# Attention, gated MLP and bilinear MLP in one kernel: six blocks of three row tiles become seven blocks of 2, 3, 3, 3, 3, 2 and 2

## The chip, the cores and the metric

The kernel runs on one core of one Trainium2 chip. The metric is the device time of one execution in microseconds (us): the median of several runs, and beside it one profiled execution, whose trace gives each instruction's start and end on each engine. TensorE is called PE in the trace (PEld is its weight loads), VectorE DVE, ScalarE ACT, GpSimd POOL, and SyncE, which issues most transfers here, SP.

## The reference, cut to what matters

```
q, k, v: (4, 8, 576, 64) fp32          # batch, heads, tokens, head size
scores = q @ k^T / 8
kth    = the 32nd largest score of each row
attn   = softmax(scores where score >= kth)
x      = (attn @ v), heads side by side # 2304 tokens x 512
h      = x @ w_in;  g = h * sigmoid(h); x2 = g @ w_out    # 512 -> 2048 -> 512
out    = ((x2 @ w1) * (x2 @ w2)) @ w3 @ w_out2            # 512 -> 1024 -> 1024 -> 512
```

The weights reach the kernel as 64-bit numbers, seen as pairs of 32-bit words.

## The kernel before, in words

The 2304 tokens are 18 row tiles of 128. They are worked in blocks of consecutive row tiles (the list BLOCKS). A block has two parts: its attention (8 heads), and then its MLP, one chain through all the weights with T = 128 x tiles columns in each matmul.

**Attention.** The (head, row tile) combinations of a block are taken two at a time: a pair. Each pair has a slot of 7 ticks in a plan. In its slot VectorE finds the 32 largest scores of both row tiles: four MAX8 (L462) and three MATCH_REPLACE8 (L466) per row tile, over 576 columns. A slot earlier TensorE has made the scores and ScalarE has copied them out (L435). A slot later ScalarE masks and takes exponentials (L482, L488), POOL normalises (L514), and when a head's row tiles are through, TensorE transposes (L569 or L572/L574) and multiplies with v (L600 or L609). A block of three row tiles has 12 slots, a block of two has 8. In blocks 0 and 1 (NATIVE: `j < 2`) attention runs in plain fp32, which needs no preparation of k and v. From block 2 on, q, k, v and the probabilities are split into a high and a low fp32r part by ScalarE and POOL, and TensorE multiplies both (two matmuls of 288 columns for half a row tile's scores, L431 and L432). The split k and v of a batch are written to DRAM if a later block needs the same batch.

**MLP.** 48 pieces of weights of 512 KB (high and low part of 128 x 512 weights) go by in order. Each product is three matmuls (L671 high x high, L672 high x low, L673 low x high). A block's MLP has 16 steps of the first part, 8 of the second: 48 pieces x 12 = 576 matmuls of T columns. The last product (w3 and the second w_out are multiplied beforehand, "folded") has 24 matmuls of 512 columns for each row tile (L792). Between the matmuls of a step the results go through tanh on ScalarE (L708), the gate on VectorE (L713), the cast to the high part on ScalarE (L685) and the subtraction of it on POOL (L686).

**Conversion.** The first time round, the weights are converted from 64-bit words: beside block 0's attention the 24 pieces to be folded, and beside block 1's attention, in step with block 0's MLP, the 48 pieces (ACT L140, L143, L136, L201, POOL L138, L156, L202, DVE L150, L153). They are written to scratch DRAM. For every later block the MLP streams all 48 pieces back (L206, issued by SP, which waits in order for a free buffer).

**Order.** The MLP of block j is spread over the ticks of the attention of block j+1. All engines take their instructions in the order that the plan gives. MLP j+1 starts only when MLP j has been issued to its end; the last MLP has no attention beside it.

Of the kernel before, what the change touches and what calls it, by code (L numbers as in the profile page):

```python
# [16 lines left out]
TOPK = 32  # L17

SHIFT = 2.0 ** -112
BLOCKS = [3, 3, 3, 3, 3, 3]  # L20
LAG = 1
WT = 3
AHEAD = 4
# [29 lines left out]
def attention_moe_moe2_kernel(  # L53
# [25 lines left out]
    scale = 1.0 / float(D) ** 0.5  # L79
    NB = len(BLOCKS)  # L80

# [17 lines left out]
    def bank(why=""):  # L99
        if not free_banks:  # L100
            raise RuntimeError(f"no bank: {sorted(held.values())}")
        b = free_banks.pop(0)
        held[id(b)] = why
        return b
# [174 lines left out]
    t0 = 0  # L279
    for n in BLOCKS:  # L280
        blocks.append((t0, n * 128))
# [18 lines left out]
    for j in range(NB):  # L300
        seq = [(j, h, i) for h in range(H) for i in range(BLOCKS[j])]
        pairs += [seq[n:n + 2] for n in range(0, len(seq), 2)]
# [234 lines left out]
    def plan_av(j, h):  # L537
# [22 lines left out]
        for kc in range(KC):  # L560
            u = {}

            def tr(u=u, kc=kc):
                u["ps"] = ps = bank("pt")
                for i in range(BLOCKS[j]):
                    p = st["p"][i]
# [350 lines left out]
```

## Time and profile before

| | |
|---|---|
| median of 3 runs | 1204.77 us (1200.64 to 1205.74) |
| the profiled execution | 1202.4 us, of which its span (first to last instruction) 1200.6 us |
| PE busy | 1149.0 us (96%), 6216 matmuls |
| DVE busy | 931.9 us (78%) |
| ACT busy | 850.1 us (71%) |
| POOL busy | 724.9 us (60%) |
| moved by DMA | 254.27 MB |

A matmul's recorded duration is longer than the time from its start to the start of the next one, since matmuls overlap. So what a matmul costs in a stream is read from two starts, not from its duration. A busy share is an average over stages that have different limits.

### The profile page before, as it was taken

What the parts mean: (1) busy time and instruction counts of PE and PEld (TensorE: products, weight loads), DVE (VectorE), ACT (ScalarE), POOL (GpSimd) and SP (SyncE); (2) the same over time, 40 slices, a digit from 0 to 9 for tenths busy, and PEclk for the clock granted to TensorE, in tenths of its full rate; (3) what the DMA queues carried; (4) which work ended last, traced back from release to release, by engine and by line L of the source; (5) the groups of instructions that cost most, each with busy time, mean ns of one, the idle gap of its engine ahead of it and who ended that gap; (6) DMA issues with size and microseconds to landing.
All of it is one profiled execution on the core that took longest, in us unless ns stands there. A gap on an engine that the chain in (4) does not pass through costs nothing.

```text
span 1200.6 us, 19669 instructions
## 1 busy us (share of the span) xinstructions
PE 1149.0 (96%) x6216; PEld 990.4 (82%) x6216; DVE 931.9 (78%) x2136; ACT 850.1 (71%) x1907; POOL 724.9 (60%) x744
## 2 busy tenths in 40 slices
PE   7799959899989999999999999999999999999997
PEld 4354535678868889989899999999999999999997
DVE  7888898999897988898889978977888998601100
ACT  6676777789897677887788778878967878642221
POOL 4454461777879367786688766677755766542231
PEclk9999989999999999999999999999999999999999
DMA  9652381678867357676678666888866775538640
GB/s 244 207 152 68 107 274 49 235 245 279 270 238 256 140 183 226 209 232 217 201 253 290 220 232 206 287 301 260 293 224 205 237 233 185 186 106 288 239 166 26
DMA packets 122504, 254.27 MB, mean 212 GB/s; under 512 B 40224, under 2 KB 63264, under 8 KB 122400
## 3 DMA queue, kind: packets, MB, share of 16 engines
q1 hardware_dynamic: 114336, 225.75, 58.3%
q10 hardware_dynamic: 8064, 27.27, 5.9%
q8 instruction: 49, 0.80, 0.3%
q14 instruction: 55, 0.45, 0.1%
HBM read 206.31 MB, written 46.66 MB: 211 GB/s over the span
## 4 chain that ended last, share of the span: by engine, by line
PE 83%; ACT 7%; DMA 4%; POOL 2%; issue 2%; DVE 1%; SPq 1%; ACTq 0%; POOLq 0%; DVEq 0%
PE bank L671 16%; PE bank L672 16%; PE bank L673 15%; PE bank L792 8%; PE bank L600 4%; PE bank L569 4%; PE bank L429 4%; PE bank L609 4%; PE bank L572 3%; PE bank L431 2%; PE bank L432 2%; PE bank L238 2%; PE bank L243 2%; DMA raw<-in_w_in_dram 1%; ACT e L482 1%
## 5 line engine op out<-in xcount | busy, mean ns | idle before, releaser
L462 DVE MAX8 top<-wk 128x8 f32<-128x576 f32 x432 | 320.5, 753 | 3.7
L686 POOL TENSOR_TENSOR gl<-gf,gh 128x384 fp32r<-128x384 f32 x144 | 148.3, 1031 | 140.0 <-ACT gh L685 131.3
L466 DVE MATCH_REPLACE8 wk<-top,wk 128x576 f32<-128x576 f32 x288 | 213.7, 744 | 0.0
L435 ACT ACTIVATE st<-bank 128x288 f32<-128x288 f32 (+1 forms) x320 | 128.1, 414 | 59.0 <-PE bank L432 30.3
L590 POOL TENSOR_TENSOR pl<-pf,ph 128x384 fp32r<-128x384 f32 x128 | 129.3, 1017 | 60.3 <-ACT ph L588 51.9
L462 DVE MAX8 top<-st 128x8 f32<-128x576 f32 x144 | 108.2, 754 | 48.6 <-ACT st L435 48.0
L671 PE MATMUL bank<-x2h,wt 128*128 128x384 f32 x384 | 131.6, 347 | 2.8 <-ACT x2h L730 2.8
L671 PE MATMUL bank<-xh,wt 128*128 128x384 f32 x384 | 130.5, 343 | 3.4 <-DVE gf L713 1.3
L672 PE MATMUL bank<-gl,wt 128*128 128x384 f32 x384 | 131.9, 344 | 1.2 <-POOL gl L686 0.7
L672 PE MATMUL bank<-x2l,wt 128*128 128x384 f32 x384 | 130.6, 340 | 1.3 <-POOL x2l L731 1.0
L673 PE MATMUL bank<-x2h,wt 128*128 128x384 f32 x384 | 129.4, 337 | 0.0
L673 PE MATMUL bank<-gh,wt 128*128 128x384 f32 x384 | 129.1, 336 | 0.0
L673 PE MATMUL bank<-xh,wt 128*128 128x384 f32 x384 | 129.0, 336 | 0.0
L672 PE MATMUL bank<-xl,wt 128*128 128x384 f32 x384 | 128.9, 336 | 0.0
L713 DVE SCALAR_TENSOR_TENSOR gf<-th,bank 128x384 f32<-128x384 f32 x96 | 52.3, 548 | 81.3 <-ACT th L708 77.1
L488 ACT ACTIVATE e<-e,nb 128x576 f32<-128x576 f32 x144 | 111.5, 779 | 0.0
L482 ACT ACTIVATE e<-st,nt 128x576 f32<-128x576 f32 x144 | 105.0, 777 | 8.3 <-DVE nt L474 6.5
L466 DVE MATCH_REPLACE8 wk<-top,st 128x576 f32<-128x576 f32 x144 | 106.7, 744 | 0.0
L156 POOL TENSOR_TENSOR w<-w,raw 128x512 f32<-128x512 f32 x48 | 66.5, 1386 | 59.8 <-DVE w L150 21.2
L685 ACT CAST gh<-gf 128x384 fp32r<-128x384 f32 x144 | 74.6, 519 | 39.3 <-DVE gf L780 24.3
L587 ACT COPY pf<-bank 128x384 f32<-128x384 f32 (+1 forms) x160 | 77.4, 484 | 33.6 <-PE bank L572 26.8
L514 POOL TENSOR_SCALAR e<-e,rc 128x640 f32<-128x640 f32 x96 | 75.8, 802 | 36.5 <-DVE rc L498 32.8
(95 smaller groups left out, 2974.9 us busy)
## 6 DMA issues: line engine op xcount, KB each, us to landing
wt<-scr SPq DMA_DIRECT2D x240, 512.0 KB, 4.2
scr<-wt ACTq DMA_DIRECT2D x48, 512.0 KB, 4.0
raw<-in_w_dram SPq DMA_DIRECT2D x24, 512.0 KB, 5.1
k<-kk SPq DMA_DIRECT2D x16, 576.0 KB, 5.1
kk<-k SPq DMA_DIRECT2D x16, 576.0 KB, 5.0
raw<-in_w3T_dram SPq DMA_DIRECT2D x16, 512.0 KB, 4.5
raw<-in_w_in_dram SPq DMA_DIRECT2D x16, 512.0 KB, 5.4
raw<-in_w_out_dram SPq DMA_DIRECT2D x16, 512.0 KB, 5.1
```

What stands on the lines that cost most here:

```text
L435: nc.scalar.activation(out=tiles[n][r0:r1, m, cs], in_=ps[r0:r1, 0:HS], func=ACTF.Copy, scale=scale)
L462: nc.vector.max(out=st["top"][:, i, r * 8:r * 8 + 8], in_=st["s" if r == 0 else "wk"][:, i])
L466: nc.vector.match_replace(out=st["wk"][:, i], in_to_replace=st["top"][:, i, r * 8:r * 8 + 8], in_values=st["s" if r == 0 else "wk"][:, i], ...
L482: nc.scalar.activation(out=e[:, 0:S], in_=st["s"][:, i], func=ACTF.Prelu, bias=st["nt"][:, i:i + 1], alpha=BELOW)
L488: nc.scalar.activation(out=e, in_=e, func=ACTF.Exp, bias=st["nb"][:, i:i + 1], accum_out=st["sm"][:, i, 0:1])
L587: nc.scalar.copy(out=pf[f], in_=u["ps"][f, 0:T])
L590: nc.gpsimd.tensor_sub(out=pl[f], in0=pf[f], in1=ph[f])
L671: nc.tensor.matmul(ps, lhsT=wh, rhs=rh, start=first, stop=False)
L672: nc.tensor.matmul(ps, lhsT=wh, rhs=rl, start=False, stop=False)
L673: nc.tensor.matmul(ps, lhsT=wl, rhs=rh, start=False, stop=last)
L686: nc.gpsimd.tensor_sub(out=u["l"], in0=full, in1=u["h"])
L792: nc.tensor.matmul(oacc[t], lhsT=a[:, ts], rhs=b[:, i, :], start=(i == 0 and x == 0), stop=(i == NI - 1 and x == 2))
```

## The change: seven blocks with their sizes in the list

The list of block sizes is changed; everything else follows from it through the same code. Blocks 0, 5 and 6 have two row tiles (T = 256), blocks 1 to 4 have three (T = 384). Blocks 0 and 1, the ones in plain fp32, have five row tiles together in place of six.

```
-BLOCKS = [3, 3, 3, 3, 3, 3]
+BLOCKS = [2, 3, 3, 3, 3, 2, 2]
```

## Rows read from the trace of the kernel before

**Rows 1.** The page: busy time, and the span in 40 slices.
```profile
PE 1149.0 (96%) x6216; PEld 990.4 (82%) x6216; DVE 931.9 (78%) x2136; ACT 850.1 (71%) x1907; POOL 724.9 (60%) x744
...
PE   7799959899989999999999999999999999999997
...
DVE  7888898999897988898889978977888998601100
```

**Rows 2.** Busy time by stage: start:end, length, each engine, clock, DMA share, GB/s.
```profile
7.00:428.00 421.00, 389.56 (x1737) 264.11 (x1736) 375.27 (x791) 317.46 (x666) 244.13 (x241) 0.97 0.62 197
428.00:590.00 162.00, 159.30 (x939) 151.67 (x938) 143.14 (x346) 129.07 (x302) 119.48 (x124) 1.00 0.66 211
590.00:752.00 162.00, 159.10 (x945) 152.38 (x944) 142.45 (x344) 127.76 (x303) 117.09 (x121) 1.00 0.73 243
752.00:921.00 169.00, 166.15 (x1042) 159.89 (x1041) 143.86 (x355) 134.41 (x318) 117.59 (x122) 1.00 0.77 261
921.00:1074.00 153.00, 152.19 (x899) 145.69 (x899) 114.00 (x279) 107.89 (x255) 94.62 (x99) 1.00 0.60 199
1074.00:1194.00 120.00, 119.75 (x657) 114.79 (x656) 13.15 (x24) 29.96 (x64) 31.20 (x31) 1.00 0.51 178
7.00:172.00 165.00, 149.64 (x494) 76.04 (x492) 147.47 (x322) 120.64 (x253) 83.52 (x84) 0.97 0.57 168
...
360.00:428.00 68.00, 68.00 (x379) 56.41 (x380) 54.07 (x119) 44.71 (x96) 40.99 (x40) 1.00 0.58 192
805.00:815.00 10.00, 10.00 (x70) 9.97 (x69) 10.00 (x28) 8.34 (x22) 6.47 (x7) 1.00 1.01 388
```

**Rows 3.** DVE's lines in 7 to 428 us: busy, mean ns, idle before.
```profile
L462 DVE MAX8 top<-wk 128x8 f32<-128x576 f32 x160 | 116.7, 748 | 0.4
L466 DVE MATCH_REPLACE8 wk<-top,wk 128x576 f32<-128x576 f32 x107 | 79.0, 742 | 0.0
...
L462 DVE MAX8 top<-st 128x8 f32<-128x576 f32 x54 | 40.3, 751 | 22.2 <-ACT st L435 22.1
L466 DVE MATCH_REPLACE8 wk<-top,st 128x576 f32<-128x576 f32 x54 | 39.8, 742 | 0.0
```

**Rows 4.** PE in order of time: 384 columns (62 in a row), then 512 (9).
```profile
1085.40 0.33 PE L671 MATMUL bank<-xh,wt 128*128 128x384 f32 x1
...
1095.97 0.33 PE L673 MATMUL bank<-xh,wt 128*128 128x384 f32 x1
...
1190.03 0.39 PE L792 MATMUL bank<-w4h,gh 128*128 128x512 f32 x1
...
1191.90 0.40 PE L792 MATMUL bank<-w4h,gl 128*128 128x512 f32 x1
```

**Rows 5.** The same view: 288 columns (8 in a row), 192 (11), transposes (6).
```profile
840.33 0.30 PE L431 MATMUL bank<-kk,qs 128*128 128x288 f32 x1
...
841.26 0.29 PE L432 MATMUL bank<-kk,qs 128*128 128x288 f32 x1
...
810.84 0.27 PE L609 MATMUL bank<-pl,vt 128*128 128x192 f32 x1
...
811.95 0.28 PE L609 MATMUL bank<-pl,vt 128*128 128x192 f32 x1
...
845.90 0.82 PE L572 MATMUL bank<-ident,e 128*128 128x128 f32 x6
846.48 0.38 PE L431 MATMUL bank<-kk,qs 128*128 128x288 f32 x1
```

**Rows 6.** One MLP step in the last stage, in order of time, all engines.
```profile
1090.77 0.33 PE L673 MATMUL bank<-xh,wt 128*128 128x384 f32 x1
...
1093.26 1.01 POOL L686 TENSOR_TENSOR gl<-gf,gh 128x384 fp32r<-128x384 f32 x1 [7.31 <-PE bank L673]
...
1096.15 0.68 PE L671 MATMUL bank<-gh,wt 128*128 128x384 f32 x3
```

**Rows 7.** DMA issues of the whole run: count, KB each, us to landing.
```profile
wt<-scr SPq DMA_DIRECT2D x240, 512.0 KB, 4.2
```

## The prediction

> **What bounds the kernel now.** I read the page first [rows 1]. PE is the busiest engine, 1149.0 of 1200.6 us, and the slices show where it is not: only in the first quarter. DVE sits at 70 to 90% until about slice 34 and then at almost nothing. So the run has a front in which PE waits, a long middle in which PE and DVE are both nearly full, and a tail of PE alone.
>
> The second view is busy time by stage, cut where the first matmul of each MLP starts [rows 2]. Until MLP 1 starts at 428 us there are 421 us in which DVE is busy 375.27, or 89%. Then come four MLPs with attention beside them (162, 162, 169 and 153 us), then MLP 5 alone (120 us), then 6.6 us to the end of the span (1200.6 - 1194). In the four middle stages PE is at 98 to 99% and DVE at 85 to 88% in the first three: the order is set by PE there. In the front it is set by DVE, which has the top-32 search of 27 slots and all the weight conversion; its longest waits are for the scores, 22.1 us [rows 3]. The front's last 68 us (360 to 428) are different: PE is busy all the time and DVE 54.07 us, because MLP 0's second part has little conversion left to wait for [rows 2].
>
> **What a matmul costs.** The starts of 62 matmuls of 384 columns lie (1095.97 - 1085.40) / 61 = 0.1733 us apart, those of 512 columns (1191.90 - 1190.03) / 8 = 0.234 [rows 4]; 288 columns take 0.133 and 192 columns 0.111 [rows 5]. From 288 up the price is in proportion to the columns; at 192 it is not (0.087 would be), so there is a floor near 0.11. The trace has no matmul of 256 columns. It lies between 0.111 and 0.133; I take 0.118, the proportional value of its nearest neighbour, 288. An MLP of 384 columns is then 576 x 0.1733 + 72 x 0.234 = 116.7 us of PE, and one of 256 columns 576 x 0.118 + 48 x 0.234 = 79.2. Six of the first kind are 700.2; four and three are 704.4. PE's MLP work hardly changes: +4 us, with bounds of -8 (0.111) and +30 (0.133), since 3 x 576 = 1728 matmuls have the new size.
>
> **The front.** The change removes one row tile from block 0: four slots of top-32 search. One slot costs DVE (116.7 + 79.0 + 40.3 + 39.8) / 27 = 10.2 us [rows 3], so 40.8 us go. The conversion stays whole. Least gain: this work alone, 40.8 us, if all waits stay. Greatest gain: four slots at the pace of block 0's stage, 165 us / 12 = 13.75 us each [rows 2], so 55, and in addition the 16 us by which PE's part of the last 68 us shrinks (MLP 0's second part there: 192 matmuls that lose 0.1733 - 0.118 each, and 24 of 512 columns that go at 0.234 each): 71. Between these I take the middle, 56: in the first part DVE is the limit, so that PE's saving is worth nothing there, and in the last 68 us, where PE is the limit, DVE at 80% has some 10 us to give before it is full itself. MLP 1 then starts at 428 - 56 = 372 us. ACT (317 us of 421) and POOL (244) get the same conversion in less time, and stay under 90%.
>
> **The middle.** MLPs 1, 2 and 3 run beside blocks of three tiles as before. Block 2 lies in one batch (162). Block 3 now spans two batches, so it loads and prepares twice as many k and v: 165, halfway to the 169 of the stage that has such a block and in addition a row tile across the border. Block 4 is like that stage: 169.
>
> MLP 4 runs beside a block of two tiles. One row tile of one head costs PE 4 x 0.133 for scores, 5 x 0.097 for transposes ((846.48 - 845.90) / 6) and a third of 9 x 0.1733 for the product with v: 1.54 us [rows 4, 5]. Eight slots of two are 24.6 us. 116.7 + 24.6 = 141.3; with the 2 to 3% that the full stages lose, 145. MLP 5, of 256 columns, has 79.2 + 24.6 - 3 (no scores of a following block) = 101, and here I add 7 us of waits. In one step the last L673 of the first product starts at 1090.77, the low part is finished at 1093.26 + 1.01 = 1094.27, and the next product starts at 1096.15: 5.38 us, or 31 matmuls, cover a chain of 3.5 [rows 6]. With 256 columns the 31 matmuls give 3.65 us, and the chain, whose operations shrink less than the columns, some 3.1. Half a microsecond is no cover when ACT and DVE have attention in their queues: one exponential late and PE stands, and with it everything behind it in its order, the next scores too. 16 steps at some 0.4 us are the 7. So 108.
>
> **The tail.** MLP 6 alone: 79.2, with the 3.3 us that 120 has over 116.7: 82.5. Then 6.6.
>
> **Sum.** 372 + 162 + 165 + 169 + 145 + 108 + 82.5 + 6.6 = 1210.1 of span, against 1200.6: +9.5. After the front the change has 838 us where the kernel before has 772.6 (1200.6 - 428); it breaks even if the front shrinks by 65.5. The profiled execution has 1.8 us around its span, so 1212. The runs' median lies 2.4 us above that execution, which is within their spread. What a measurement of this kernel can tell from no change is about 0.5%, 6 us: faster means under 1198.7, slower over 1210.8.
>
> **A rule beside this.** The page TensorE: Matmul & The Clock Gate of the Trainium skill (section Back-to-back issue gap) gives two prices. N / 2.4 + 2.5 ns would be 162.5 at 384 and 109 at 256: +1.5 us for the MLPs where my rows make it +4. Its sustained figures, about 81 ns at N = 128 and 131 at N = 512, would by a straight line be 114 and 98, an estimate that has a large fixed part and speaks against small blocks: 1728 x 98 - 1152 x 114 ns = +38 us. The rows at 288, 384 and 512 show no such fixed part, and the measured prices decide.
>
> **Rivals.**
>
> *The front gives more than the tail takes (0.25; 1190 to 1200).* PE waits for conversion in the front; if fewer matmuls there let scores come sooner, DVE's 22.1 us of waiting for scores go too. It decides from 65.5 us on. At 71 us and with no added waits in MLP 5: 1212 - 15 - 7 = 1190. For it: the 68 us that PE fills alone. Against: DVE at 89% has little to give.
>
> *The weight stream limits the last two blocks (0.18; 1220 to 1246).* All later MLPs stream 48 pieces; 240 loads become 288 [rows 7]. MLPs 5 and 6 need 96 x 0.524 = 50.3 MB, and block 6's eight heads about 1 MB each of q, k and v: 58.7 MB in 190 us, 308 GB/s. No stage before has more than 261 [rows 2]. At 261 it takes 225 us, +35; at 290, +12. Against: 10 us at 388 GB/s are there [rows 2]. The place is the first part of MLP 6, where PE would wait for pieces.
>
> *The conversion sets the front's pace (0.08; 1228).* If 24 folded pieces no longer fit beside 8 slots, the front shrinks by some 40: +16. Against: POOL is busy 58% there.
>
> *A matmul of 256 columns costs as much as one of 288 (0.04; 1238).* +26 against my 0.118. The floor at 192 speaks for something of the kind, but it lies below 0.118. The skill's sustained figures (above) are its other form, at +38.
>
> **How the numbers follow.** My forecast, 1212, stands for a front that shrinks by 50 to 64 us: 1204 to 1218, with 0.45. About half of it lies within 0.5% of the median and half above. Faster: most of the first rival, 0.24. Same: half the forecast and the rest of that rival, 0.26. Slower: the rest, 0.50. The range leaves out the last rival, the upper end of the stream's and the lowest end of the first: 1192 to 1232.
>
> **What would show it.** The first matmul of MLP 1 at 372 us. Starts of 256-column matmuls 0.118 us apart. Stage lengths of 145 for MLP 4 and 108 for MLP 5, the latter with waits of PE for L685 and L686. DVE's busy share in the front still near 90%. I am wrong if the front shrinks by over 65 us, if the 256-column price leaves 0.11 to 0.125, or if PE waits for transfers of weights at the end.

## The result, and the profile after

The changed kernel takes 1209.76 us (median of 15 runs, 1206.19 to 1219.0), the kernel before 1202.72 us (15 runs). The ratio is 1.0073, 95% interval 1.0051 to 1.0095: the change costs 0.7%. The profiled execution took 1209.91 us with a span of 1208.1. The spans of the 15 runs reach from 1204.4 us (mean granted clock 0.989) to 1217.2 (0.977), so a difference of a few us between two single traces says little.

The page of the changed kernel, busy time of the engines and then the issues of the weight transfers; the rows of before are in [rows 1] and [rows 7]:

```profile
PE 1157.2 (96%) x6896; PEld 1009.3 (84%) x6896; DVE 939.1 (78%) x2168; ACT 876.2 (73%) x2071; POOL 759.2 (63%) x828
...
wt<-scr SPq DMA_DIRECT2D x288, 512.0 KB, 4.7
```

PE has 680 matmuls more and is busy 8 us longer, in a span that is 7.5 us longer. No engine's share of the span has moved by more than 3 points: what happened is seen only by stage. Busy time by stage of the changed kernel, cut at the start of each MLP as in [rows 2] (start:end, length, then each engine, clock, DMA share, GB/s):

```profile
7.00:365.00 358.00, 330.70 (x1599) 218.65 (x1599) 321.90 (x677) 285.60 (x619) 233.51 (x230) 0.96 0.74 237
365.00:529.00 164.00, 159.14 (x936) 150.95 (x936) 145.10 (x358) 128.44 (x304) 117.97 (x124) 1.00 0.74 240
529.00:696.00 167.00, 163.93 (x1023) 157.84 (x1022) 143.00 (x348) 130.51 (x307) 119.54 (x124) 1.00 0.81 271
696.00:873.00 177.00, 171.85 (x1046) 162.87 (x1045) 148.38 (x359) 137.41 (x324) 119.79 (x127) 1.00 0.78 261
873.00:1017.00 144.00, 143.68 (x867) 139.03 (x866) 104.78 (x243) 95.98 (x252) 82.45 (x103) 1.00 0.71 242
1017.00:1122.00 105.00, 103.25 (x804) 99.15 (x803) 65.84 (x163) 73.08 (x209) 64.47 (x89) 1.00 0.77 273
1122.00:1204.00 82.00, 81.80 (x628) 78.70 (x627) 10.05 (x24) 22.09 (x59) 20.66 (x29) 1.00 0.69 257
```

The front ends at 365.1 us in place of 428: 62.9 us are won. From there to the end of the span the changed kernel needs 1208.1 - 365.1 = 843 us, the kernel before 1200.6 - 428 = 772.6: 70.4 us are lost. What moved is read from PE's column. In the front PE is busy 330.70 us in place of 389.56 [rows 2], 58.9 us less: one row tile's third of MLP 0 and that tile's attention are gone from it. Behind the front PE is busy 1157.2 - 330.70 = 826.5 us in place of 1149.0 - 389.56 = 759.4, 67.1 us more. So PE's work grows by 8.2 us and its idle time falls by 0.7 (50.9 us in place of 51.6): the 7.5 us between the spans are as much as PE's added work.

What a matmul of 256 columns costs can now be read. PE in order of time in the last stage, the first and the last of 44 such matmuls without a pause:

```profile
1129.83 0.28 PE L671 MATMUL bank<-xh,wt 128*128 128x256 f32 x1
...
1134.99 0.28 PE L671 MATMUL bank<-xh,wt 128*128 128x256 f32 x1
```

(1134.99 - 1129.83) / 43 = 0.120 us: 0.002 more than I took, and no fixed cost of weight loads on top. At this price the MLPs are 7.7 us more work than before, where I had 4. The 67.1 us behind the front can be put together by an estimate: 44 us are the MLPs behind the front at these prices, some 12 the moved tile's attention at the prediction's prices, and 10.5 the growth of PE's busy time in the stages of MLP 2 (163.93 against 159.10) and MLP 3 (171.85 against 166.15), 66.5 in all.

The floor near 0.11 that I read from 192 columns does not hold for smaller matmuls. Two of 64 columns in the changed kernel take 0.14 us together, from 810.64 to 810.78:

```profile
810.64 0.19 PE L609 MATMUL bank<-ph,vt 128*128 128x64 f32 x1
810.67 0.27 PE L609 MATMUL bank<-pl,vt 128*128 128x64 f32 x1
810.78 0.42 PE L672 MATMUL bank<-x2l,wt 128*128 128x384 f32 x1
```

### The profile page after: what moved, and what is told of

The parts are those of the page before. It is cut to its first block, busy times and chain, and to the rows that moved or that the text cites. A ratio compares the mean times of both kernels' runs of the same rounds, so it can differ in the third digit from the quotient of the medians.

```text
span 1208.1 us, 21716 instructions
## 1 busy us (share of the span) xinstructions
PE 1157.2 (96%) x6896; PEld 1009.3 (84%) x6896; DVE 939.1 (78%) x2168; ACT 876.2 (73%) x2071; POOL 759.2 (63%) x828
## 4 chain that ended last, share of the span: by engine, by line
PE 72%; ACT 11%; DVE 6%; DMA 5%; POOL 3%; issue 3%; SPq 1%; ACTq 0%; POOLq 0%; DVEq 0%
PE bank L671 14%; PE bank L672 14%; PE bank L673 13%; PE bank L792 7%; PE bank L609 4%; PE bank L600 3%; PE bank L569 3%; PE bank L429 3%; PE bank L572 3%; PE bank L238 2%; DVE wk L466 2%; PE bank L243 2%; PE bank L431 2%; ACT e L488 2%; DVE top L462 2%
## 5 line engine op out<-in xcount | busy, mean ns | idle before, releaser
L686 POOL TENSOR_TENSOR gl<-gf,gh 128x384 fp32r<-128x384 f32 (+1 forms) x168 | 153.2, 915 | 122.5 <-ACT gh L685 105.0
L590 POOL TENSOR_TENSOR pl<-pf,ph 128x384 fp32r<-128x384 f32 (+1 forms) x160 | 143.8, 906 | 78.2 <-ACT ph L588 67.8
L671 PE MATMUL bank<-xh,wt 128*128 128x384 f32 (+1 forms) x448 | 143.5, 324 | 7.8 <-ACT st L435 5.2
L671 PE MATMUL bank<-x2h,wt 128*128 128x384 f32 (+1 forms) x448 | 141.7, 323 | 2.1 <-ACT pn L580 1.3
L672 PE MATMUL bank<-x2l,wt 128*128 128x384 f32 (+1 forms) x448 | 141.4, 317 | 0.9 <-POOL x2l L731 0.8
L672 PE MATMUL bank<-gl,wt 128*128 128x384 f32 (+1 forms) x448 | 139.3, 323 | 1.6 <-POOL gl L686 1.1
L672 PE MATMUL bank<-xl,wt 128*128 128x384 f32 (+1 forms) x448 | 140.3, 314 | 0.2 <-POOL xl L631 0.2
L673 PE MATMUL bank<-xh,wt 128*128 128x384 f32 (+1 forms) x448 | 140.4, 314 | 0.0
L673 PE MATMUL bank<-x2h,wt 128*128 128x384 f32 (+1 forms) x448 | 140.2, 314 | 0.0
L673 PE MATMUL bank<-gh,wt 128*128 128x384 f32 (+1 forms) x448 | 136.1, 316 | 0.0
L685 ACT CAST gh<-gf 128x384 fp32r<-128x384 f32 (+1 forms) x168 | 79.0, 472 | 52.3 <-DVE gf L780 34.4
L587 ACT COPY pf<-bank 128x384 f32<-128x384 f32 (+3 forms) x200 | 88.1, 440 | 36.9 <-PE bank L572 22.6
```

The costliest lines, as they stand in the source:

```text
L587: nc.scalar.copy(out=pf[f], in_=u["ps"][f, 0:T])
L590: nc.gpsimd.tensor_sub(out=pl[f], in0=pf[f], in1=ph[f])
L671: nc.tensor.matmul(ps, lhsT=wh, rhs=rh, start=first, stop=False)
L672: nc.tensor.matmul(ps, lhsT=wh, rhs=rl, start=False, stop=False)
L673: nc.tensor.matmul(ps, lhsT=wl, rhs=rh, start=False, stop=last)
L686: nc.gpsimd.tensor_sub(out=u["l"], in0=full, in1=u["h"])
```

## The experiments

All start from the changed kernel unless said otherwise. MLP 1's start, which ends the front, is the start of its first matmul in the trace; it is 365.1 us in the changed kernel. Two traces of a front in which the program does the same differ: it ends at 428.0 us in the kernel before and at 424.0 in e1_small_last, and at 365.1 in the changed kernel and 366.9 in e3_half_stream, where the granted clock is 0.94 in place of 0.96. So a difference of 4 us in the front's end shows nothing. The front of e3_half_stream:

```profile
7.00:367.00 360.00, 335.66 (x1601) 222.05 (x1600) 322.11 (x677) 286.25 (x620) 234.29 (x230) 0.94 0.72 230
```

**1. Where the small blocks stand.** The same seven sizes, all small ones at the end, and all in front.

```
-BLOCKS = [2, 3, 3, 3, 3, 2, 2]
+BLOCKS = [3, 3, 3, 3, 2, 2, 2]     # e1_small_last
+BLOCKS = [2, 2, 2, 3, 3, 3, 3]     # e2_small_first
```

Expected of e1_small_last:

> Blocks of 3, 3, 3, 3, 2, 2, 2: seven blocks with the sizes of the change, but all small ones at the end; block 0 and so the front are those of the kernel before. My theory (the time is PE's work plus PE's waiting; only a small first block shortens the front): MLP 1 starts at 428 us as before, the tail is shorter by 33 us but the work in the middle longer by as much, and the split into seven costs 4 us of PE work and some 3 to 8 us of waiting: span 1205 to 1213. Rival (a short last block is a gain in itself, since the tail has PE alone): 1165 to 1190.

Expected of e2_small_first:

> Blocks of 2, 2, 2, 3, 3, 3, 3: the same sizes, all small ones in front; plain fp32 attention for four row tiles in place of five. My theory: two row tiles' search less before MLP 1 than in the kernel before, PE work 16 us less than in the changed kernel (one row tile fewer in plain fp32); MLP 1 starts at 315 to 330 us (365 in the changed kernel), and with PE's waiting as in the changed kernel the span is 1190 to 1200. Rival (the seventh pass through the weights is what costs): as slow as the changed kernel, 1206 to 1212.

e1_small_last takes 1222.58 us, ratio 1.0168 (1.0147 to 1.0189), span 1216.6. The front is that of the kernel before (MLP 1 at 424.0), so the rest costs 1216.6 - 424.0 = 792.6 us where the kernel before has 772.6: 20 us, which is also the difference of the medians. Splitting the end into two-tile blocks is thus no gain in itself, which refutes the rival, and it is dearer than my 4 + 3 to 8 us. Its stages, MLP 2 to MLP 5:

```profile
585.00:755.00 170.00, 165.91 (x987) 158.15 (x986) 147.36 (x354) 136.70 (x325) 123.90 (x130) 1.00 0.74 248
755.00:912.00 157.00, 154.48 (x953) 148.71 (x952) 109.10 (x255) 106.75 (x274) 94.30 (x114) 1.00 0.78 268
912.00:1021.00 109.00, 105.29 (x821) 100.86 (x820) 93.23 (x227) 82.08 (x231) 68.61 (x95) 1.00 0.86 308
1021.00:1130.00 109.00, 104.92 (x810) 99.92 (x809) 67.33 (x170) 76.69 (x217) 67.23 (x94) 1.00 0.78 269
```

MLP 2 runs over the same block sizes as in the kernel before and takes 170 us, not 162 [rows 2]. What differs is that the block after it, whose first slots already lie in this stage, has two tiles, and 42 matmuls more fall into it (987 against 945). That this block's slots cause the 8 us is my reading. The stage of MLP 3, of three tiles beside a two-tile block across a batch border, takes 157 where my price for such a stage was 145.

e2_small_first takes 1241.76 us, ratio 1.0336 (1.0307 to 1.0365), and so misses my 1190 to 1200 by far. Its trace is of the slowest of its six runs (1250.08). Front and the two stages behind it:

```profile
7.00:357.00 350.00, 304.67 (x1413) 198.36 (x1413) 296.39 (x597) 265.99 (x589) 245.19 (x234) 0.92 0.72 233
357.00:496.00 139.00, 126.72 (x906) 117.00 (x905) 89.33 (x226) 98.17 (x266) 91.57 (x115) 0.95 0.87 293
496.00:631.00 135.00, 126.83 (x911) 117.57 (x911) 130.69 (x337) 113.04 (x284) 97.92 (x110) 0.99 0.78 268
```

A second row tile less before MLP 1 gives 8 us, not the 40 to 55 that the first one's price would make. DVE is busy 25 us less than in the changed kernel's front and PE 26, POOL 12 us more, and the clock that PE is granted is 0.92 in place of 0.96. This was the first sign that the front does not follow one engine's work.

**2. The weight stream.** Half the bytes: only the high half of each piece is streamed, and it is used where the low half belongs.

```
-        nc.sync.dma_start(out=t.bitcast(FP32), in_=scr[k])
+        nc.sync.dma_start(out=t[:, 0].bitcast(FP32), in_=scr[k][:, 0])
-            nc.tensor.matmul(ps, lhsT=wl, rhs=rh, ...)
+            nc.tensor.matmul(ps, lhsT=wl if j == 0 else wh, rhs=rh, ...)
```

> The changed kernel, but MLPs 1 to 6 stream only the high half of each piece of weights (256 KB in place of 512 KB) and use it also where the low half belongs; the number of matmuls and of transfers is the same, the moved bytes fall by about 75 MB. My theory (the stream is hidden): span 1204 to 1209, no stage shorter by over 4 us. Rival (the stream's contention is what the middle stages lost, 177 us for MLP 3 in place of 169): 1190 to 1200, MLP 3's stage at 168 or less.

1207.66 us, ratio to the kernel before 1.0049 (1.0031 to 1.0067). The stage of MLP 3 is no shorter than before the edit although more than a quarter of the traffic is gone:

```profile
697.00:876.00 179.00, 173.77 (x1051) 164.90 (x1050) 149.29 (x359) 138.50 (x326) 120.51 (x128) 0.99 0.57 187
```

187 GB/s in place of 261, 179 us in place of 177. From MLP 6's start to the end it takes 86.8 us in place of 86.5, at 132 GB/s in place of 257: the stream is hidden, and the rival that the seventh pass through the weights costs by its transfers has fallen.

**3. VectorE's work in the front.** One round of the search less in blocks 0 and 1, which keeps 24 scores there in place of 32.

```
-        NR = TOPK // 8
+        NR = TOPK // 8 - (pr[0][0] < 2)     # and TOPK -> 8 * NR below
```

> The changed kernel with three rounds of the top-k search in place of four for blocks 0 and 1 (it keeps 24 scores there): VectorE has about 2.8 us less to do in each of 20 slots, 56 us. My theory (VectorE sets the front): MLP 1 starts 35 to 56 us earlier, at 310 to 330 us, and the span falls as much, to 1150 to 1175. Rival (the conversion's chain through ScalarE, POOL and the transfers sets it): MLP 1 at 350 or later, span over 1190.

1203.95 us, span 1199.2, MLP 1 at 355.5. Front:

```profile
7.00:355.00 348.00, 330.40 (x1598) 216.24 (x1597) 275.66 (x561) 285.76 (x623) 233.67 (x230) 0.97 0.76 244
```

DVE is busy 46 us less and the front is 10 us shorter (the medians differ by 6). VectorE alone does not set the front; the theory of the prediction falls here, and the numbers are those of the rival, the conversion's chain. But PE's busy time in the front, 330.40 us of 348, is that of the changed kernel (330.70 of 358), and at 95% it leaves little to win. So there were two theories from here: the conversion, and PE's own work.

**4. TensorE's work in the front, less and more.** MLP 0 without the third matmul of each product, and with the first one made twice.

```
+            if j > 0:                                      # e5_two_matmuls; the one ahead of it then ends the sum
                 nc.tensor.matmul(ps, lhsT=wl, rhs=rh, ...)
```

```
             nc.tensor.matmul(ps, lhsT=wh, rhs=rh, start=first, stop=False)
+            if j == 0:                                     # f2_four_matmuls
+                nc.tensor.matmul(ps, lhsT=wh, rhs=rh, start=False, stop=False)
```

> The changed kernel, but MLP 0 leaves out the third matmul of each product (low weights x high activations): 192 matmuls of 256 columns less, 192 x 0.1195 = 23 us of TensorE work less in the front, nothing else. New theory (TensorE's own work sets most of the front): MLP 1 starts at 342 to 347 us in place of 365, span 1185 to 1190. Rival (VectorE, ScalarE and POOL with search and conversion set it): MLP 1 at 358 or later, span 1200 or more.

> The changed kernel with the first matmul of each of MLP 0's products made twice: 192 matmuls of 256 columns more, 23 us of TensorE work more in the front (the mirror image of e5_two_matmuls). Theory (TensorE's work is hidden in the front, and what it adds raises the granted clock, 0.94 from 116 to 311 us, toward 1): MLP 1 at 362 to 372, span 1204 to 1214, with a higher granted clock. Rival (TensorE's work does set the front, and in e5_two_matmuls something else took the gain): MLP 1 at 382 to 390, span 1225 to 1232.

e5_two_matmuls takes 1213.93 us, ratio 1.0084 (1.0052 to 1.0116), MLP 1 at 370.8: 23 us of TensorE's work are gone and the front is no shorter, but 6 us longer. f2_four_matmuls takes 1222.36 us, ratio 1.0168 (1.0137 to 1.0199), MLP 1 at 376.2: 23 us more work, 11 us more time. The two fronts, e5_two_matmuls first:

```profile
7.00:371.00 364.00, 322.93 (x1408) 204.54 (x1407) 315.69 (x675) 284.02 (x616) 233.93 (x229) 0.92 0.72 233
```

```profile
7.00:376.00 369.00, 347.52 (x1791) 238.74 (x1790) 327.64 (x687) 289.01 (x625) 235.00 (x232) 0.98 0.72 231
```

The column to look at is the granted clock: 0.92, 0.96 in the changed kernel, 0.98. PE has two levels, 2.4 and 1.2 GHz; a mean of 0.92 over 364 us means 2 x 0.08 x 364 = 58 us at the lower one, 0.96 over 358 us 29, and 0.98 over 369 us 15. In these three fronts PE stands idle for 41, 27 and 21 us, so the clock falls with more idle time. In e5_two_matmuls PE spends 29 us more at half speed, and what it does there takes up to twice as long: up to 15 of the 23 us go back this way. That the clock falls after PE has stood idle is what the Trainium skill says too (TensorE: Matmul & The Clock Gate, The HAM clock gate: the default state is throttled, and activity releases it); the three rows agree in the direction. The order is not strict: the front of before has 31 us of idle time and 0.97. Over whole runs, all four of e5_two_matmuls have a lower clock (0.968 to 0.975) than any of the changed kernel's (0.977 to 0.989), while those of f2_four_matmuls (0.983 to 0.991) overlap with them. The rest of the 23 us, and the 6 on top (little more than the spread of two traces), I cannot place. e5_two_matmuls ends where its rival had it (358 or later), f2_four_matmuls between its two ranges: TensorE's added work is half paid for, its removed work not at all.

**5. ScalarE and POOL.** Without the sign operations; without the low halves; with all signs on VectorE.

```
-        if not SIGN_BITS(n, fold):                         # f1_no_sign
-            nc.scalar.activation(out=h, in_=h, func=ACTF.Sign)
```

```
-            nc.gpsimd.tensor_sub(out=t[:, 1], in0=w, in1=t[:, 0])   # e6_no_low, on e3_half_stream;
...          # MLP 0 uses the high half too, and only that half is written to scratch
```

```
-SIGN_BITS = lambda n, fold: not fold and n % 2 == 0
+SIGN_BITS = lambda n, fold: not fold                       # f4_sign_on_dve
```

> The changed kernel without the 48 sign operations of ScalarE in the conversion (the multiplication takes the raw high word in their place): 48 x 0.68 = 33 us of ScalarE work less in the front, half of it beside MLP 0. Theory (ScalarE, 86% busy from 116 to 311 us, is what sets the front): MLP 1 starts at 332 to 348 us in place of 365, span 1175 to 1192. Rival (no engine's work alone sets it; the front is a net of short waits between engines that take their work in the plan's order, as the earlier runs with less VectorE, TensorE or POOL work suggest): MLP 1 at 353 to 368, span over 1195.

> As e3_half_stream, and in addition the conversion makes no low half at all: 48 subtractions of 1.35 us on POOL (65 us of its 230 us of work in the front) and half of the bytes written to scratch are left out, and MLP 0 too uses the high half where the low belongs; the number of matmuls is the same. New theory (TensorE's work sets the front): MLP 1 starts at 358 to 367 us, as in e3_half_stream (367). Rival (the conversion's pace, with POOL as its slowest member): 310 to 345.

> The changed kernel, the same result, with the signs of all 48 converted pieces put in by VectorE (24 more operations of about 1 us there) in place of ScalarE's sign and POOL's multiplication for every second one (24 x 0.68 = 16 us less for ScalarE, 24 x 1.36 = 33 us less for POOL). If ScalarE is the limit: MLP 1 at 350 to 358, span 1192 to 1202. If VectorE is, as the prediction had it: MLP 1 at 375 to 385, span 1218 to 1228. If neither: 362 to 370.

f1_no_sign: 1208.89 us, ratio 1.0057 (1.0033 to 1.0082), MLP 1 at 365.9. ScalarE is busy 256.80 us in the front in place of 285.60, and the front is as long as it was. e6_no_low: 1216.09 us, ratio 1.0115 (1.0087 to 1.0144), MLP 1 at 370.5, where e3_half_stream has 366.9: 65 us less on POOL bring nothing. Their fronts, f1_no_sign first:

```profile
7.00:366.00 359.00, 334.68 (x1600) 221.36 (x1600) 316.64 (x675) 256.80 (x568) 230.72 (x229) 0.95 0.74 236
```

```profile
7.00:371.00 364.00, 332.60 (x1603) 222.06 (x1602) 309.16 (x679) 286.29 (x619) 163.57 (x182) 0.95 0.63 192
```

f4_sign_on_dve: 1220.82 us, ratio 1.0161 (1.0118 to 1.0204), MLP 1 at 378.8, 13.7 us later than in the changed kernel. VectorE's sign operations in the changed kernel, then the same line and the front here:

```profile
L153 DVE SCALAR_TENSOR_TENSOR w<-raw,w 128x512 uint32<-128x512 uint32 x24 | 23.6, 983 | 0.0
```

```profile
L153 DVE SCALAR_TENSOR_TENSOR w<-raw,w 128x512 uint32<-128x512 uint32 x48 | 39.6, 824 | 0.0
...
7.00:379.00 372.00, 343.73 (x1616) 228.32 (x1615) 330.19 (x701) 274.02 (x600) 203.57 (x207) 0.94 0.71 229
```

The 24 added operations cost VectorE 16 us in this line and 8 us in its busy time of the whole front (330.19 against 321.90), and the front is 13.7 us longer, although ScalarE and POOL have less to do. Front and span (1219.8) lie in the ranges that were set for VectorE as the limit. The clock of 0.94 may have a part in it. So VectorE's work counts in full when it is added, and for about a fifth of itself when it is removed (run 3).

**6. All three lighter at once.**

```
+ NR as in e4_topk3, no Sign as in f1_no_sign, and
-        else:
-            nc.gpsimd.tensor_tensor(out=w, in0=w, in1=r[:, :, 1].bitcast(FP32), op=ALU.mult)
```

> The changed kernel with all three conversion engines lighter at once in the front: three rounds of search in place of four in blocks 0 and 1 (VectorE 56 us less), no sign operations (ScalarE 33 us less) and no multiplication by the sign (POOL 48 x 1.37 = 66 us less). TensorE's work is unchanged. If the front is a net of waits between these engines, their sum counts where one alone did not: MLP 1 at 315 to 340, span 1160 to 1180. If TensorE's own work is the floor (295 us of it at back-to-back prices before 365 us): MLP 1 at 340 to 356, span 1180 to 1200.

1193.33 us, ratio 0.9919 (0.9889 to 0.9949), MLP 1 at 347.9. Front:

```profile
7.00:348.00 341.00, 325.37 (x1603) 215.56 (x1602) 265.61 (x561) 261.37 (x574) 167.15 (x180) 0.97 0.77 247
```

147 us of work on the three engines are gone (56 on VectorE, 24 on ScalarE, 66 on POOL), and the front is 17 us shorter: PE is now busy 325.37 of 341 us, 95%, with everything else under 80%. It comes out where the second expectation put it, with PE's work as the floor under the front; that no engine but PE is near its limit fits this, but a run with less work for PE in this state was not made.

**7. Fewer row tiles in plain fp32; more cover for the chain.**

```
-NATIVE = lambda j: j < 2
+NATIVE = lambda j: j < 1                                   # e7_native_one_block
```

```
-LAG = 1
+LAG = 2                # e8_lag_two; the pool keeps its three buffers
```

> The changed kernel with plain fp32 attention in block 0 alone: two row tiles in place of five. Three row tiles move from plain fp32 (about 28 us of TensorE work each) to split fp32r (about 13): 47 us less TensorE work, but beside the conversion ScalarE gets some 35 us and POOL some 65 us more. New theory in its strong form (only TensorE counts in the front): span 1160 to 1180. Rival (ScalarE and POOL are nearly full beside the conversion, so that what TensorE saves is waited for): 1200 or more, with the gain of TensorE showing as its waiting in MLP 0's stage.

> The changed kernel with the second product two steps behind the first in place of one (same buffers), so that the chain tanh, gate, cast, subtraction has twice the cover. Theory of the prediction (MLP 5, with 256 columns, waits some 6 us for this chain): its stage falls from 104 to 98 to 101 us, and the stages of MLPs 1 to 3 lose some of their 13 to 21 us of waiting; span 1193 to 1204. Rival (the waits in those stages are for attention's results, which this does not touch): 1205 to 1212, MLP 5 at 103 to 105.

e7_native_one_block takes 1245.37 us, ratio 1.0356 (1.0327 to 1.0386), MLP 1 at 406.9. Three row tiles move from plain fp32 to split fp32r. MLP 0's stage:

```profile
149.00:407.00 258.00, 185.18 (x1022) 162.98 (x1023) 225.07 (x464) 217.46 (x471) 250.23 (x227) 0.81 0.79 265
```

Here one engine does set the stage: POOL, 250.23 of 258 us, with the splitting of attention on top of the conversion. PE waits, and its clock falls to 0.81. The block of plain fp32 beside the conversion is there for a reason.

e8_lag_two takes 1220.85 us, ratio 1.0152 (1.0125 to 1.0179). MLP 5's stage is 105 us as before the edit (104), as the rival had it, and MLP 3's is 178 in both. The time is above both expectations, since the front is 11 us longer (MLP 1 at 376.4), for a reason that stays open. With the same three buffers the two steps may have waited for a buffer in place of the chain, so this run alone would not clear the chain. The changed kernel's own trace does. These are all of PE's listed waits in MLP 5's stage, 1017 to 1122 us, and none is for L685 or L686:

```profile
PE bank L609 <- ACT ph L588: 0.5, 1, 0.5
PE bank L671 <- ACT o L797: 0.5, 1, 0.5
PE bank L671 <- ACT ph L588: 0.5, 1, 0.5
```

## Why the prediction was right, point by point

The forecast was 1212 us; the span came to 1208.1 where the sum had 1210.1. The sign and the size were right, but in part by luck: the front and MLPs 4 to 6 came out some 14 us shorter than their terms and MLPs 1 to 3 some 12 us longer, and these errors cancel. The sum's largest term was near in size for a reason that the runs bore out only in part.

**The front.** I had it shrink by 56 us, and it shrank by 62.9. The step that failed is its reason, "in the front it is set by DVE", with "PE's saving is worth nothing there". Run 3 takes 46 us from DVE and wins 10; in run 5 DVE's added work counts in full. So DVE is a limit, but another lies close behind it, and runs 4 and 5 show that taking work from PE, ScalarE or POOL alone wins nothing. What I had passed over stands in [rows 2]: in the front of before PE is busy 389.56 of 421 us, more than DVE's 375.27. The change takes work from both, 59 us of PE's busy time and 53 of DVE's (375.27 - 321.90), and the front gets shorter by about as much. Run 6, with PE at 95% and the others under 80%, fits PE as the limit behind DVE, some 10 to 17 us away.

That taking from these two together is what it needs is my reading; a run that lightens PE and DVE alone was not made. Run 4 says that such a run could show less than the sum, by the clock, and e2_small_first speaks against the reading in its simple form: it takes a further 26 us from PE and 25 from DVE, and its front is only 8 us shorter. The other reading, a net of short waits between engines that work in the plan's order, is not excluded. In the changed kernel's front ScalarE waits 29.5 us for raw weights, while SP, which loads them, waits 112 us for buffers that VectorE and POOL free; a run with more buffers was not made.

**The price of a matmul.** 0.118 was taken and 0.120 measured; the rival that 256 columns cost as much as 288 (0.133) is out, and with it the estimate that I had worked out from the Trainium skill's sustained figures (TensorE: Matmul & The Clock Gate, Back-to-back issue gap).

**The middle.** MLPs 1 and 2 took 164 and 166.5 us for my 162 and 165. MLP 3 took 177.8 for my 169, the largest error behind the front. It is not the stream (run 2), and it is no accident of one trace: the stage takes 178.9 us in e3_half_stream and 177.6 in e8_lag_two. In run 1 the stage ahead of the first two-tile block was longer by 8 us as well, with 42 matmuls more in it. In the changed kernel the number of matmuls in this stage is nearly the same as before (1046 and 1042), so the cause of its 9 us stays open. MLP 4 took 143.8 for 145. MLP 5 took 104.3 for 108: I had added 7 us of waiting for the chain from tanh to the low part. The stage is 3 us over the sum without it, and PE's waits there name the chain nowhere (run 7). The cover of half a microsecond was enough.

**The tail.** MLP 6 and the end took 86.5 us for 89.1. Its weights arrived in time at 257 GB/s: PE is busy 81.80 of 82 us.

**The rivals.** "The front gives more than the tail takes" needed 65.5 us by my sum and would have needed 70 by the measured one; 62.9 came. The stream was hidden. The conversion does not set the front's pace in the changed kernel, but it was near: with three tiles' attention more to split, POOL does (run 7), and in e2_small_first, with POOL 12 us busier, the second tile did not bring its worth.

So PE's work stays, and a smaller first block only moves it behind the front. PE's idle time in the front hardly falls: 31.4 us before (421 - 389.56), 27.3 in the changed kernel (358 - 330.70). Small blocks at the end alone cost 20 us (run 1: medians of 1222.58 against 1202.76), and putting one of them first gives back 13 of these (1209.76). The only version faster than the kernel before, f3_all_lighter, leaves out part of the computation.

## What to carry to other kernels

Before a front or a stage is put down to one engine, read the busy share of every engine in it. If two are near 90%, taking work from one alone may show little, while work that is added to one can count in full. Shifting work between stages gains only what it takes out of the idle time of the engine that bounds the whole, so that sum should be made for that engine first: here PE's work grew by 8.2 us and the span by 7.5. A shorter last block looks like a gain in the tail, but it is only one if the work that leaves the tail falls into idle time somewhere else.

## What the runs showed of the hardware

Taking 192 matmuls out of a stretch in which PE already paused now and then went with a lower granted clock (0.92 in place of 0.96) and won nothing; adding 192 went with 0.98 and cost half their price. The front without either edit shows 0.94 to 0.96, so only the fall is clear of the spread. With POOL as the limit the clock fell to 0.81 over 258 us. In this stretch added work on TensorE was cheaper than its price, and leaving work out was worth less.

VectorE's 128x512 operation that puts in the sign (L153 of the changed kernel) took 0.82 us in the fronts where POOL was busy 45 to 55% of the time (e6_no_low, f3_all_lighter, f4_sign_on_dve), 0.98 at 65% (the changed kernel) and 1.11 at 83% (e7_native_one_block). So POOL's load shows in VectorE's time as well; the reason was not tested.
